# Window attention with routed experts on one core: half of the first slot's row transposes at the end of step 11, a shorter slot table placed ahead of the routing, no warming products in step 0, weight pieces from step 5

## The chip, the cores and the metric

The kernel runs on one core of one Trainium2 chip. The metric is the device time of one execution in microseconds (us); the median of three runs stands for the kernel. The engines are named as the profile names them: PE multiplies matrices (PEld loads its weights), DVE, ACT and POOL are the vector, scalar and general engines, and SP issues DMAs.

## The reference, cut to what matters

```python
# attention: batch 8, heads 8, seq 576, head_dim 64, window 64
scores = 1/sqrt(64) * q @ k.T
scores = where((0 <= row - col) & (row - col < 64), scores, -1e9)
attn = exp(scores - max); attn = attn / (sum(attn) + 1e-9)
x = (attn @ v)                       # 4608 tokens x 512
# one expert of 8 for every token
logits = x @ w_gate + modality_bias[modality_id]
e = argmax(logits); gate = softmax(logits)[e]
out = gate * (relu(x @ w1[e]) @ w2[e])   # w1: 512 x 1024, w2: 1024 x 512
```

## The kernel before, in words

The 4608 tokens are 36 pairs of 64-row blocks. A loop of 40 steps runs the attention as a software pipeline: step s holds the values (`values`, tile av) and the routing logits (`logits`) of earlier pairs, the scores (`scores`, tile sp) and row minima (`minima`, tile mn) of pair s, the transposes of the probabilities of pair s-1 (`probs_t`, PSUM to SBUF as pT by ACT), the transposes of the attention rows (`x_t`, xaT), the exponentials of pair s (`exps`, ACT), and the transposes of the next group's heads (`heads_t`, copied as kT and qT). All engines but the DMA rings work through orders that this code writes out by hand; the order of the calls is the order in each engine's queue.

Every second step a group of two pairs is routed: `route1` to `route3` put small DVE operations on a list, `routing`, and two indirect DMAs of POOL (`scatter`, line 735) write each token's row to a DRAM scratch tensor, xs_scratch, by expert. `tick` takes operations off that list, or off a second one, `queue`, which holds the *table*: tiny DVE operations on one partition that work out which rows the next expert *slot* may take. `plan` queues such a table for two slots after the groups named in `EARLY`; the first plan comes at the end of step 9 (group 2).

An expert slot is 256 token rows of one expert. Its work is cut into pieces by the generator `slot_pieces`, and from step `FIRST` = 12 on a step has four places for a piece (`gap`). The pieces of the first slot are: `x_part` 0 and 1 (four 128x128 transposes each of the slot's rows xt, line 255, then a split into a high part xh by ACT and a low part xl by DVE, lines 193 and 194), `first` k, i (12 products each into half of a PSUM bank, line 280; after i = 1 ACT makes hh and DVE makes hl of the bank, lines 288 and 289), and `second` (six products each, line 302). While the attention runs, `bank` gives every `first` the one bank em, and `x_part` 0 as well. So `first` 1, 0 can't write em before hh and hl of k = 0 have read it. `fetch` takes the next slot off `todo`: it ticks the table up to the operation that gives the slot's row number, SP reads that number (`load_slot`, line 202) and loads the rows into xt (line 204). Such a load is ordered behind the scatters of its groups.

The two most used experts' weights are kept as pairs Whi and Wlo. Each call of `weights` takes one piece a stage on: a load of 256 KB into a tile y by SP (lines 101 and 105), `split_hi` by ACT (line 112), `split_lo` by DVE in the call after it (line 117). 32 pieces are needed; `first` 0 and 1 use the first four of them. Before, the calls begin in step 3 (`WEIGHTS`).

In step 0, `keep_warm(4)` and later `keep_warm(3)` are products of zeros into the bank em (line 846), whose results nobody reads. The second of them stands behind the transposes of the first heads, which also go into em, and which DVE copies out as kT (line 563).

When the 40 steps are over, the pieces left run alone: loads, splits and products of further slots, and at the end one slot of 128 rows.

Of the kernel before, what the change touches and what calls it, by code (L numbers as in the profile page):

```python
# [8 lines left out]
F32 = mybir.dt.float32  # L9
# [4 lines left out]
ALU = mybir.AluOpType  # L14
# [5 lines left out]
P = 128  # L20
# [6 lines left out]
def tile_window_attn_moe(  # L27
# [12 lines left out]
    nc = tc.nc  # L40
# [13 lines left out]
    TP = 2 * P  # L54
# [6 lines left out]

    EARLY = ((2, (0, 1)), (4, (0, 1)), (6, (0, 1)), (8, (0, 1)), (9, (1, 2)), (10, (1, 2)), (11, (1, 2)),
             (12, (0, 2)), (13, (0, 2)), (15, (0, 2)))
    WEIGHTS = 3
    FIRST = 12


# [54 lines left out]
    queue = []  # L122
    issued = [0]
    n_raw = [0]
    routing = []
# [9 lines left out]
    def queued():  # L135
        return issued[0] + len(queue)

    def ts(pool, nm, in0, s1, op0, s2=None, op1=ALU.bypass, dtype=F32, out=None):
        t = pool.tile(list(in0.shape), dtype, name=nm) if out is None else out
        queue.append(lambda: nc.vector.tensor_scalar(  # L140
            out=t, in0=in0, scalar1=s1, scalar2=s2, op0=op0, op1=op1))
        return t

    def stt(pool, nm, in0, scalar, in1, op0, op1):
        t = pool.tile(list(in0.shape), F32, name=nm)
        queue.append(lambda: nc.vector.scalar_tensor_tensor(
            out=t, in0=in0, scalar=scalar, in1=in1, op0=op0, op1=op1))
        return t

    def tt(pool, nm, in0, in1, op, dtype=F32, out=None):  # L150
        t = pool.tile(list(in0.shape), dtype, name=nm) if out is None else out
        queue.append(lambda: nc.vector.tensor_tensor(out=t, in0=in0, in1=in1, op=op))
        return t
# [6 lines left out]
    def tiles_of(pool, nm, c, up, size):  # L160

        i = ts(pool, nm + "_i", c, float(size - 1) if up else 0.0, ALU.add, dtype=I32)
        sh = pool.tile(list(c.shape), I32, name=nm + "_s")
        queue.append(lambda: nc.vector.tensor_single_scalar(
            out=sh, in_=i, scalar=size.bit_length() - 1, op=ALU.arith_shift_right))
        return ts(pool, nm, sh, 0.0, ALU.add)
# [61 lines left out]
    def run_later():  # L228
        while later:
            later.pop(0)()  # L230

    def fetch():
        if fetched:
            return fetched.pop(0)
        row, late, buf, whichever, need = todo.pop(0)
        assert late is not None or not pads
        assert late is None or late in scattered
        tick(need - issued[0], table=True)
        nb = 1 if whichever == NANY else 2
        return dict(xt=load_slot(row, late, nb), buf=buf, any=whichever, nb=nb)  # L240
# [191 lines left out]
    def gap(it, wait=False):  # L432

        if next(it, "end") != "end" and not wait:
            run_later()
            tick()
# [40 lines left out]

    PARTS = ((K0, K1), (Q0, Q1))
    AHEAD = range(1, 8)
    WARM = 4, 3  # L480

    n_tp = [0]

    def turn_bank(s):

        i = n_tp[0]
        n_tp[0] += 1
        if s < FIRST and i % 5 > 1:
            return ps_m.tile([P, 512], F32, name=("em", "y0", "y1")[i % 5 - 2])
        return ps_t.tile([P, 512], F32, name="tp")  # L490
# [162 lines left out]
    def logits(p, lt):  # L653
        G, j = divmod(p, GB)
        xaT = st.pop((p, "xT"))
        for c in range(NC1):
            for i in range(2):
                cols = slice(c * P + i * W64, c * P + (i + 1) * W64)
                nc.tensor.matmul(  # L659
                    out=lt[i * W64:(i + 1) * W64, 0:E], lhsT=xaT[:, cols], rhs=wg[:, c, :],  # L660
                    start=(c == 0), stop=(c == NC1 - 1))
        if j == 0:
            st[G, "lg"] = small.tile(sh3, F32, name="lg")
        nc.vector.tensor_tensor(
            out=st[G, "lg"][:, j, :], in0=lt[:, 0:E], in1=bias_sel[:, p, :], op=ALU.add)
# [100 lines left out]
    def plan(T, xs_, cnt):  # L766

        nm = "e"
        xs_ = slice(*xs_)
        n = per_expert(pl, nm + "_n", tiles_of(pl, nm + "_f", cnt, False, TP), xs_)  # L770
        n = tt(pl, nm + "_av", n, used[-1][:, xs_], ALU.subtract)
        take = ts(pl, nm + "_take", n, 1.0, ALU.min)
        row = stt(pl, nm + "_first", used[-1][:, xs_], 2.0, base2[:, xs_], ALU.mult, ALU.add)
        row = tt(pl, nm + "_at", row, take, ALU.mult)
        rows = ts(tab, f"rows_{len(used)}", row, float(DUMMY), ALU.add, dtype=I32)
        new = pl.tile([1, 2], F32, name=nm + "_used")
        if xs_.stop - xs_.start < 2:
            ts(pl, nm, used[-1], 0.0, ALU.add, out=new)
        tt(pl, nm, used[-1][:, xs_], take, ALU.add, out=new[:, xs_])
        used.append(new)  # L780
        for i, x in enumerate(range(xs_.start, xs_.stop)):
            todo.append((rows[0:1, i:i + 1], f"scatter_after_{T}", x, None, queued()))

    def choose():

# [57 lines left out]
    def keep_warm(n):  # L843
        em = ps_m.tile([P, 512], F32, name="em")
        for _ in range(n):
            nc.tensor.matmul(out=em, lhsT=idle[:, 0:P], rhs=idle[:, 0:512], start=True, stop=True)

    keep_warm(WARM[0])
    ident_r = const.tile([P, P], F32R, name="ident_r")
    ident = ident_r.bitcast(F32)  # L850
    ident_0 = epool.tile([P, 512], F32, name="hl", bufs=2)[:, 0:P]
# [125 lines left out]
    for s in range(NPR + 4):  # L977
        j = s % GB
        for f, args in at.pop(s, ()):
            f(*args)  # L980
        n_tick = 6 if s < FIRST else 5
        n_gap = 0 if s < FIRST else 4
        G = s // GB + 1
        heads = PARTS[j] if G < NG else ()
        R = (s - 5) // GB if s >= 5 and j == 1 else -1
        if 1 <= s < FIRST:
            swap_upper(s - 1)

        if 2 <= s < NPR + 2:
            values(s - 2)  # L990
            values_out(s - 2)
        if 3 <= s < NPR + 3:
            logits(s - 3, turn_bank(s))
            if (s - 3) % GB == GB - 1:
                route1((s - 3) // GB)
        if s < NPR:
            scores(s)
            minima(s)
        if 1 <= s <= NPR:
            if s >= FIRST:  # L1000
                swap_upper(s - 1)
            swap_v(s - 1)
            for a in range(2):
                probs_t(s - 1, a, turn_bank(s))
            sums(s - 1)
        if s < NPR:
            exps(s, (0, 1))
        if s == 0:
            first_pair(1, (both[:1], both[1:]))
            keep_warm(WARM[1])  # L1010
            cast_bias()
        if n_gap > 0:
            gap(it, True)
        if 2 <= s < NPR + 2:
            x_t(s - 2, turn_bank(s))
        run_later()
        tick(2)
        if s == FIRST - 1:
            fetched.append(fetch())
        if s < NPR:  # L1020
            exps(s, (2, 3, 4))
        if n_gap > 0:
            if s < FIRST + 4 or s % 2:
                weights(s)
            gap(it, True)
        if heads:
            tp = turn_bank(s)
            heads_t(G, *heads[0], tp)
            heads_out(tp, G, *heads[0], nc.vector.tensor_copy)
        run_later()  # L1030
        tick(n_tick)
        cnt = None
        if R >= 0:
            tp = turn_bank(s)
            rk = route2(R, tp)
            if R == NG - 1 or any(R == T for T, _ in EARLY):
                cnt = counts_out(tab if R == NG - 1 else pl, counts(R, tp))
            route3(R, rk)
        if s < NPR:
            exps(s, (5, 6, 7))  # L1040
        if n_gap > 2:
            if FIRST < s < FIRST + 3:
                weights(s)
            gap(it, True)
        if heads:
            tp = turn_bank(s)
            heads_t(G, *heads[1], tp)
            heads_out(tp, G, *heads[1], nc.scalar.copy if heads[1] == K1 else nc.vector.tensor_copy)
        run_later()
        tick(n_tick)  # L1050
        if s == WEIGHTS:
            load_weights()
        if s >= WEIGHTS:
            weights(s)
        if n_gap > 3:
            gap(it, True)
        run_later()
        if s == 1:
            select_bias()
        if s == 4:  # L1060
            nc.sync.dma_start(out=xs_blk[DUMMY:DUMMY + 2].rearrange("b p c -> p b c"), in_=padrow)
        for T, xs_ in EARLY:
            if T == R:
                plan(T, xs_, cnt)
    tick(len(routing))
    tick(len(queue))

# [264 lines left out]
```

## Time and profile before

| what | value |
| --- | --- |
| median of 3 runs | 640.25 us (639.64 to 640.69) |
| the profiled execution | 639.68 us, of which its span is 637.9 us |
| granted clock in the page's rows | 9 of 9 tenths in all 40 slices |
| bytes moved by DMA | 88.07 MB, 138 GB/s over the span |

A row of the timeline gives the start and the length in us, the engine, the line, the operation, out<-in, how many were merged, and in brackets how long the engine stood idle before it and what ended that. In the windows view each row is a stretch with every engine's busy time. Starts of a step below are the starts of its scores on PE. The order views list an engine's instructions as they stand in its queue; no time is in them.

### The profile page before, as it was taken

The numbers are of one execution on the slowest core, as the hardware profiler recorded it, in microseconds if no ns is written. First come the engines' busy times: TensorE is split into PE (matmuls) and PEld (weight loads), VectorE is DVE, ScalarE is ACT, GpSimd is POOL, SyncE is SP. The second block draws the span as 40 slices with busy tenths as digits, with TensorE's granted clock in tenths as the row PEclk, the third lists the DMA queues.
The fourth block names the chain that finished last, engine by engine and source line by source line (L and its number), as shares of the span: only waits on it lengthen the run. The fifth ranks groups of instructions, "written<-read, shape, count | busy, mean of one in ns | idle before, by whom it ended". The sixth has DMA issues, their size and how long they took to land.

```text
span 637.9 us, 17255 instructions
## 1 busy us (share of the span) xinstructions
PE 618.2 (97%) x6508; PEld 555.2 (87%) x6509; DVE 366.2 (57%) x1489; ACT 299.4 (47%) x933; POOL 136.6 (21%) x315
## 2 busy tenths in 40 slices
PE   6999789999999999999999999999999999999996
PEld 4888688989898889889888899998999899989986
DVE  3899968776777766666654364213224624667611
ACT  3899876656656555646462111111112513554411
POOL 6333322132222320321222121011001101101202
PEclk9999999999999999999999999999999999999999
DMA  9999664775466543453312026312232723677300
GB/s 182 222 240 238 167 187 126 191 194 158 133 166 192 141 134 85 134 150 85 101 50 101 33 100 245 116 39 67 67 132 80 244 75 104 214 244 241 106 5 32
DMA packets 138773, 88.07 MB, mean 138 GB/s; under 512 B 116618, under 2 KB 116672, under 8 KB 138560
## 3 DMA queue, kind: packets, MB, share of 16 engines
q1 hardware_dynamic: 130112, 67.44, 40.2%
q0 software_dynamic: 5888, 18.93, 7.9%
q8 instruction: 52, 0.85, 0.6%
q10 hardware_dynamic: 2688, 0.58, 0.5%
q14 instruction: 33, 0.27, 0.1%
HBM read 67.49 MB, written 23.91 MB: 143 GB/s over the span
## 4 chain that ended last, share of the span: by engine, by line
PE 50%; DVE 0%; ACT 0%; issue 0%; POOL 0%; POOLq 0%; ACTq 0%
PE y L302 23%; PE em L280 13%; PE sp L280 10%; PE tp L440 1%; PE y L353 1%; PE av L634 1%; PE em L255 1%; PE tp L255 1%; PE sp L328 0%; PE em L328 0%; PE tp L659 0%; PE sp L582 0%; DVE xa L642 0%; ACT ss L608 0%; POOL out_dram L366 0%
## 5 line engine op out<-in xcount | busy, mean ns | idle before, releaser
L302 PE MATMUL y<-Whi,hh 128*128 128x512 f32 x288 | 118.7, 412 | 0.0
L608 ACT ACTIVATE ss<-ss,mn 128x128 f32<-128x128 f32 x288 | 112.6, 398 | 3.4 <-DVE mn L596 3.4
L302 PE MATMUL y<-Whi,hl 128*128 128x512 f32 x288 | 112.8, 392 | 0.0
L302 PE MATMUL y<-Wlo,hh 128*128 128x512 f32 x288 | 112.8, 392 | 0.0
L280 PE MATMUL em<-xh,Whi 128*128 128x256 f32 x400 | 102.9, 292 | 1.2 <-ACT xh L193 0.7
L280 PE MATMUL em<-xh,Wlo 128*128 128x256 f32 x400 | 98.1, 279 | 0.0
L289 DVE SCALAR_TENSOR_TENSOR hl<-em,hh 128x512 fp32r<-128x512 f32 x50 | 34.5, 690 | 91.4 <-ACT hh L288 91.3
L313 POOL DMA_INDIRECT out_dram<-y,id x36 | 37.3, 1037 | 222.6 <-DVE y L310 140.5
L280 PEld LDWEIGHTS em<-xh,Whi 128*128 128x128 f32 x400 | 75.4, 189 | 2.6 <-ACT xh L193 0.9
L280 PEld LDWEIGHTS em<-xh,Wlo 128*128 128x128 f32 x400 | 75.3, 188 | 0.9
L288 ACT ACTIVATE hh<-em 128x512 fp32r<-128x512 f32 x50 | 29.6, 591 | 93.0 <-PE em L280 89.1
L596 DVE CUSTOM_DVE_ANT_0 ss<-sp,masks 128x128 f32<-128x128 f32 x288 | 63.6, 286 | 11.4 <-PE sp L582 11.4
L617 ACT COPY pT<-tp 128x512 f32<-128x512 f32 x57 | 31.6, 589 | 76.3 <-PE tp L440 76.3
L302 PEld LDWEIGHTS y<-Whi,hl 128*128 128x128 f32 x288 | 54.1, 188 | 12.3
L280 PE MATMUL em<-xl,Whi 128*128 128x256 f32 x400 | 63.1, 279 | 0.0
L302 PEld LDWEIGHTS y<-Whi,hh 128*128 128x128 f32 x288 | 54.1, 188 | 7.3
L302 PEld LDWEIGHTS y<-Wlo,hh 128*128 128x128 f32 x288 | 54.3, 189 | 7.0
L608 ACT ACTIVATION_READ_ACCUMULATOR ss<-ss,mn 128x1 f32 x288 | 56.0, 195 | 0.0
L735 POOL DMA_INDIRECT xs_scratch<-xa,idx x36 | 36.3, 1010 | 84.8 <-DVE lm L678 26.9
L280 PEld LDWEIGHTS em<-xl,Whi 128*128 128x128 f32 x400 | 53.8, 188 | 0.0
L289 DVE SCALAR_TENSOR_TENSOR hl<-sp,hh 128x512 fp32r<-128x512 f32 x22 | 15.2, 692 | 60.8 <-ACT hh L288 60.8
L288 ACT ACTIVATE hh<-sp 128x512 fp32r<-128x512 f32 x22 | 13.1, 597 | 76.6 <-PE sp L280 76.6
(249 smaller groups left out, 1266.5 us busy)
## 6 DMA issues: line engine op xcount, KB each, us to landing
xt<-xs_scratch SPq DMA_DIRECT2D x18, 514.0 KB, 4.1
vo<-in_v_dram SPq DMA_DIRECT2D x32, 256.0 KB, 4.2
y<-in_moe_w_dram SPq DMA_DIRECT2D x32, 256.0 KB, 3.8
vo<-in_moe_w_dram SPq DMA_DIRECT2D x24, 256.0 KB, 3.8
ss<-in_moe_w_dram SPq DMA_DIRECT2D x24, 256.0 KB, 3.8
xs_scratch<-xs_scratch SPq DMA_DIRECT2D x8, 514.0 KB, 6.3
pT<-in_moe_w_dram SPq DMA_DIRECT2D x16, 256.0 KB, 3.5
qk<-in_k_dram SPq DMA_DIRECT2D x14, 256.0 KB, 4.5
```

The lines of the kernel that those rows point to most:

```text
L255: nc.tensor.transpose(out=tp[:, n * P:(n + 1) * P].bitcast(F32R), in_=xt[:, t, c * P:(c + 1) * P].bitcast(F32R), identity=ident_r)
L280: nc.tensor.matmul(out=hb[:, i * TP:(i + 1) * TP], lhsT=w[buf][:, c0:c0 + P], rhs=x[:, c * TP:(c + 1) * TP], start=(n == 0), stop=(n == le ...
L288: nc.scalar.activation(out=hh, in_=hb, func=AF.Relu),
L289: nc.vector.scalar_tensor_tensor(out=hl, in0=hb, scalar=0.0, in1=hh.bitcast(F32), op0=ALU.max, op1=ALU.subtract)))
L302: nc.tensor.matmul(out=sl["y", t], lhsT=h[:, i * TP + t * P:i * TP + (t + 1) * P], rhs=w[buf][:, c0:c0 + DM], start=(k == 0 and n == 0), s ...
L313: ins = nc.gpsimd.indirect_dma_start(out=out, out_offset=bass.IndirectOffsetOnAxis(ap=sl["id"][:, t:t + 1], axis=0), in_=y, in_offset=None ...
L353: nc.tensor.matmul(out=yp[:, cols], lhsT=sl["h", n][lo][:, c * P:(c + 1) * P], rhs=w[buf][:, c0 + cols.start:c0 + cols.stop], start=(m == ...
L440: nc.tensor.transpose(out=out_, in_=in_, identity=ident[p0:p0 + n, p0:p0 + n])
L596: nc.vector.tensor_tensor_reduce(out=ss[a][:, hp, :], in0=sp[a][:, hp * P:(hp + 1) * P], in1=mask, scale=-1.0 / 8.0, scalar=3.0e38, op0=AL ...
L608: nc.scalar.activation(out=ss[a][:, hp, :], in_=ss[a][:, hp, :], func=AF.Exp, bias=mn[:, h:h + 1], scale=-1.0, accum_out=sm[:, h:h + 1])
L617: nc.scalar.copy(out=pT, in_=pp)
L735: ins = nc.gpsimd.indirect_dma_start(out=xs, out_offset=bass.IndirectOffsetOnAxis(ap=idx[:, j:j + 1], axis=0), in_=xg[j], in_offset=None)
```

## The change

- The three warming products of step 0 go (`WARM`).
- The calls of `weights` begin in step 5 instead of 3; steps 12 and 15 get one more call each.
- `plan` is worked out with fewer operations: it compares the expert's count with 256 times the number of slots used, instead of first making whole slots of it. The row number comes ahead of the count of used slots. For the plan of step 9 the operations up to the row number are issued at once, where before they were ticked behind the routing's, in steps 10 and 11.
- `fetch` for the first slot stands at the start of step 11 and `x_part` 0 of that slot at its end; all later pieces come one place earlier. The logits of step 12 go to another bank.
- In the odd steps from 13 on the rest of the routing list is issued at the end of the step.

On PE, at the end of step 11 and in step 12, this stood before (ss are probabilities, xt the slot's rows, xa attention rows, Whi_64 heads of q and k, which lie in memory that later holds weights; Whi_65 and xh the first product's operands):

```order
L440 MATMUL tp<-ident_r,ss 128x128 x8
L255 MATMUL em<-ident_r,xt 128x128 x4
L440 MATMUL tp<-ident_r,xa_101 128x128 x4
L255 MATMUL tp<-ident_r,xt 128x128 x4
L440 MATMUL tp<-ident_r,Whi_64 128x128 x4
L280 MATMUL em<-xh,Whi_65 128x256
```

And this stands there now, at the end of step 11, with the values (av) of the next step behind it:

```order
L706 MATMUL em<-oh,ones 128x8
L440 MATMUL y_1731<-ident_r,Whi_64 128x128 x4
L255 MATMUL em<-ident_r,xt 128x128 x4
L634 MATMUL av<-ve,pT 64x64
L634 MATMUL av<-vo,pT 64x64
```

The first four transposes of the slot's rows moved from behind step 12's scores to a place ahead of step 12's values.

On PE at the end of step 12 the last products of `first` 0, 1 were followed before by the values of step 13:

```order
L280 MATMUL em<-xh,Whi_65 128x256
L280 MATMUL em<-xh,Wlo_66 128x256
L280 MATMUL em<-xl,Whi_65 128x256 x4
L634 MATMUL av<-ve,pT 64x64
L634 MATMUL av<-vo,pT 64x64
```

Now they are followed by one set of head transposes and then by `first` 1, 0, which writes the same bank:

```order
L280 MATMUL em<-xl,Whi_65 128x256 x4
L440 MATMUL tp<-ident_r,Whi_64 128x128 x4
L280 MATMUL em<-xh,Whi_65 128x256
L280 MATMUL em<-xh,Wlo_66 128x256
L280 MATMUL em<-xh,Whi_65 128x256
```

`first` 1, 0 came after the values, logits, scores and probabilities of step 13 before, and comes ahead of all of them now.

On DVE, the table of the first plan (names beginning with e_) stood in step 10 before, behind the routing's last operation and ahead of a split; four more operations of it followed in step 11:

```order
L691 TENSOR_REDUCE oh<-oh 128x8
L140 TENSOR_SCALAR e_f_i<-cnt 1x8
L164 TENSOR_SCALAR e_f_s<-e_f_i 1x8
L140 TENSOR_SCALAR e_f<-e_f_s 1x8
L152 TENSOR_TENSOR e_n_p<-sel_68,e_f 1x8
L157 TENSOR_REDUCE e_n<-e_n_p 1x1
L152 TENSOR_TENSOR e_av<-e_n,used_220 1x1
L140 TENSOR_SCALAR e_take<-e_av 1x1
L146 SCALAR_TENSOR_TENSOR e_first<-used_220,base_69 1x1
L117 TENSOR_TENSOR Wlo_66<-y,Whi_65 128x512
```

Now it stands at the end of step 9, behind the scatter's index and a split, and ahead of step 10's first operations:

```order
L747 CAST idx<-dst 128x2
L117 TENSOR_TENSOR Wlo_66<-y,Whi_65 128x512
L146 SCALAR_TENSOR_TENSOR e_first<-used_220,base_69 1x1
L152 TENSOR_TENSOR e_n_p<-sel_68,cnt 1x8
L157 TENSOR_REDUCE e_n<-e_n_p 1x1
L146 SCALAR_TENSOR_TENSOR e_av<-used_220,e_n 1x1
L146 SCALAR_TENSOR_TENSOR e_at<-e_av,e_first 1x1
L140 TENSOR_SCALAR rows_1471<-e_at 1x1
L512 COPY ve<-vo 64x512
L640 RECIPROCAL rs<-rs 128x8
```

The row number is there after six operations in step 9 instead of ten in steps 10 and 11; two operations for the slots used stay in step 10.

```diff
-    WEIGHTS = 3
+    WEIGHTS = 5
     FIRST = 12
...
-    WARM = 4, 3
+    WARM = 4
...
         xs_ = slice(*xs_)
-        n = per_expert(pl, nm + "_n", tiles_of(pl, nm + "_f", cnt, False, TP), xs_)
-        n = tt(pl, nm + "_av", n, used[-1][:, xs_], ALU.subtract)
-        take = ts(pl, nm + "_take", n, 1.0, ALU.min)
-        row = stt(pl, nm + "_first", used[-1][:, xs_], 2.0, base2[:, xs_], ALU.mult, ALU.add)
-        row = tt(pl, nm + "_at", row, take, ALU.mult)
+        was = used[-1][:, xs_]
+        row = stt(pl, nm + "_first", was, 2.0, base2[:, xs_], ALU.mult, ALU.add)
+        n = per_expert(pl, nm + "_n", cnt, xs_)
+        n = stt(pl, nm + "_av", was, -float(TP), n, ALU.mult, ALU.add)
+        row = stt(pl, nm + "_at", n, float(TP), row, ALU.is_ge, ALU.mult)
         rows = ts(tab, f"rows_{len(used)}", row, float(DUMMY), ALU.add, dtype=I32)
+        for i, x in enumerate(range(xs_.start, xs_.stop)):
+            todo.append((rows[0:1, i:i + 1], f"scatter_after_{T}", x, None, queued()))
...
-        tt(pl, nm, used[-1][:, xs_], take, ALU.add, out=new[:, xs_])
         used.append(new)
-        for i, x in enumerate(range(xs_.start, xs_.stop)):
-            todo.append((rows[0:1, i:i + 1], f"scatter_after_{T}", x, None, queued()))
+        new = new[:, xs_]
+        queue.append(lambda: nc.vector.scalar_tensor_tensor(
+            out=new, in0=n, scalar=float(TP), in1=was, op0=ALU.is_ge, op1=ALU.add))
...
             f(*args)
+        if s == FIRST - 1:
+            fetched.append(fetch())
...
-            logits(s - 3, turn_bank(s))
+            logits(s - 3, turn_bank(s) if s != FIRST else ps_m.tile([P, 512], F32, name="y0"))
...
             first_pair(1, (both[:1], both[1:]))
-            keep_warm(WARM[1])
             cast_bias()
         if n_gap > 0:
             gap(it, True)
+        if s == FIRST:
+            run_later()
...
-        if s == FIRST - 1:
-            fetched.append(fetch())
...
         if n_gap > 0:
-            if s < FIRST + 4 or s % 2:
+            if FIRST < s < FIRST + 4 or s % 2:
                 weights(s)
             gap(it, True)
+        if s == FIRST:
+            run_later()
+            weights(s)
...
         if n_gap > 2:
-            if FIRST < s < FIRST + 3:
+            if FIRST <= s < FIRST + 4:
                 weights(s)
             gap(it, True)
...
-        if n_gap > 3:
+        if n_gap > 3 or s == FIRST - 1:
             gap(it, True)
         run_later()
+        if s >= FIRST and j == 1:
+            tick(len(routing))
...
                 plan(T, xs_, cnt)
+                if not fetched and s < FIRST:
+                    tick(todo[0][-1] - issued[0], table=True)
```

More of the change, by code (lines that the diff above doesn't have):

```diff
@@ L846, in keep_warm @@
             nc.tensor.matmul(out=em, lhsT=idle[:, 0:P], rhs=idle[:, 0:512], start=True, stop=True)
-    keep_warm(WARM[0])
+    keep_warm(WARM)
     ident_r = const.tile([P, P], F32R, name="ident_r")
```

## The prediction

> **What bounds the kernel now.** I read the page first, then the busy time by step in windows, then PE's timeline at the start and around step 12, and last POOL's, SP's, ACT's and DVE's timelines at the places where PE waits.
>
> ```profile
> span 637.9 us, 17255 instructions
> PE 618.2 (97%) x6508; PEld 555.2 (87%) x6509; DVE 366.2 (57%) x1489; ACT 299.4 (47%) x933; POOL 136.6 (21%) x315
> ```
>
> PE is busy for 618.2 of 637.9 us. The change takes nothing but three products off PE, so what it can give lies in PE's 19.7 idle us and in stretches where PE goes at less than its pace. The windows, one for each step (columns: length; busy PE, PEld, DVE, ACT, POOL with counts; granted clock; DMA share; GB/s), show where those are.
>
> ```profile
> 26.89:31.76 4.87, 4.87 (x105) 4.51 (x101) 4.03 (x22) 4.72 (x19) 0.83 (x2) 1.00 0.86 222
> 42.08:47.45 5.37, 4.94 (x105) 4.51 (x101) 5.07 (x28) 5.37 (x23) 3.76 (x6) 1.00 0.98 244
> 70.33:76.87 6.54, 5.20 (x107) 4.59 (x104) 6.11 (x37) 5.45 (x21) 0.41 (x2) 1.00 0.39 106
> 76.87:89.33 12.46, 9.53 (x136) 8.14 (x132) 9.36 (x42) 9.52 (x33) 5.19 (x10) 1.00 0.75 216
> 89.33:100.01 10.68, 10.68 (x145) 9.62 (x141) 7.94 (x36) 6.78 (x23) 0.89 (x3) 1.00 0.37 102
> ```
>
> Step 3 (first row) is PE's alone. In step 6 (42.08) ACT is busy all the time and PE and DVE nearly so. In step 11 (70.33) DVE leads and PE is idle for 1.3 us; step 12 (76.87) holds 2.9 us of idle PE; from step 13 on PE has no gap. Everything that stands before 89 us moves the end one for one, everything later only if it makes PE wait.
>
> The start, on PE (columns: start, length, engine, line, operation, what, count, idle before):
>
> ```profile
> 8.71 1.98 PE L582 MATMUL sp<-kT,qT 64*64 64x128 f32 x32 [0.61 <-POOL hl L864]
> 11.96 0.63 PE L440 MATMUL y<-ident_r,qk 64*128 64x64 f32 x4
> 13.29 0.58 PE L846 MATMUL em<-hh 128*128 128x512 bf16 x1 [0.69 <-DVE X_mx L157]
> 14.10 0.63 PE L846 MATMUL em<-hh 128*128 128x512 bf16 x1 [0.22 <-issue]
> 14.52 1.06 PE L440 MATMUL y<-ident_r,Whi 128*128 128x128 f32 x4
> 16.36 1.99 PE L582 MATMUL sp<-kT,qT 64*64 64x128 f32 x32
> 18.28 0.81 PE L440 MATMUL tp<-ident_r,ss 128*128 128x128 f32 x4
> 18.92 0.60 PE L440 MATMUL em<-ident_r,ss 128*128 128x128 f32 x4
> 21.58 1.10 PE L582 MATMUL sp<-kT,qT 64*64 64x128 f32 x32
> ```
>
> The same 32 score products take 1.99 us at 16.36 and 1.10 us at 21.58, four transposes 1.06 and later 0.60: PE goes at about half pace until some 18.7 us, though the clock in the windows' rows reads 1.00 throughout. The pace changed after PE had been without a gap since 14.10, for 4.6 us.
>
> **The change, part by part.** The sum goes against the profiled execution, 639.68 us (639.68 - 637.9 = 1.8 outside the span), which lies 0.57 under the median of 640.25.
>
> *No warming products.* They wait for em and hold PE from 12.59 (11.96 + 0.63) to 14.52, 1.9 us. SP's last issue of the heads that the next transposes read, and its time to landing:
>
> ```profile
> 4.90 1.91 SPq L533 DMA_DIRECT2D Whi<-in_k_dram  x1
> DMA to landing us min/median/max: 6.3/6.3/6.3
> ```
>
> They are in memory at 11.2, so those transposes can start at 12.59. Without the products PE runs from 8.71 with no gap through the transposes and the scores of step 1. If the pace changes after as long a run as it did, 4.6 us, that is at 13.3 instead of 18.7, and the transposes and scores up to there are up to 0.9 us shorter each (1.99 - 1.10 for the scores). The bound on that side is 1.9 + 0.9 = 2.8. What is late next is POOL:
>
> ```profile
> 24.73 0.60 POOL L506 COPY ve<-vo 64x512 f32<-64x512 f32 x1
> ```
>
> This copy, which the second pair's values need, stands behind POOL's bias work, and that behind DVE's copies of the heads, which don't move as far as PE does; my estimate is that this gives about one such copy back, 0.6. So 2.2. If the pace still changes only at 18.7, eight probability transposes come before that and lose 2 x (1.06 - 0.60) = 0.9, and the gain is 1.0. I take -2.2, nearer to the early change because the run without a gap is longer than the one that sufficed. In steps 3 and later the gain persists, as PE there has nothing to wait for.
>
> The Trainium skill, "TensorE: Matmul & The Clock Gate", Part 1, says that the array runs at half clock until one free-running window of about 3.4 us was busy throughout; the trace agrees, and by that rule the change of pace would come between 12.1 and 15.5 us, and the gain would be -2.5 rather than -2.2, 637.9 in all.
>
> *Weights from step 5.* Two splits leave the crowded steps 5 and 6, which are alike, and return in steps 12 and 15. The groups of operations by line, from 30 to 60 us, give their price (count | busy, mean ns):
>
> ```profile
> L112 ACT CAST Whi<-y 128x512 fp32r<-128x512 f32 x5 | 3.2, 633 | 0.0
> L117 DVE TENSOR_TENSOR Wlo<-y,Whi 128x512 fp32r<-128x512 f32 x4 | 2.7, 684 | 0.0
> ```
>
> ACT has 2 x 0.5 to 0.6 us less, DVE 2 x 0.7. PE itself needs 4.87 (step 3) of step 6's 5.37, so at most 0.5 a step can be had: between 0 and -1.0, I take -0.6. Two 256 KB loads leave the stretch where the DMA share is near 1.0; that helps the heads' loads and costs nothing.
>
> *The shorter table.* Before, twelve operations lie in steps 10 and 11 (eight and four):
>
> ```profile
> 70.33 0.15 DVE L140 TENSOR_SCALAR e_f_i<-cnt 1x8 int32<-1x8 f32 x1
> 71.53 0.14 DVE L146 SCALAR_TENSOR_TENSOR e_first<-used,base 1x1 f32<-1x1 f32 x1
> 75.42 0.14 DVE L152 TENSOR_TENSOR e_at<-e_first,e_take 1x1 f32<-1x1 f32 x1
> 75.84 0.15 DVE L152 TENSOR_TENSOR e_used<-used,e_take 1x1 f32<-1x1 f32 x1
> ```
>
> They take 1.3 + 0.6 us of DVE. Six operations at the same pitch now delay step 10 by 0.9 and two more by 0.2. Of the first 1.3 that leaves 0.2, by which the end of step 11 comes earlier on PE; the row number is there at the end of step 9 instead of behind 75.42.
>
> *The early rows and transposes.* With the number early, the load of the rows waits for the scatters of its group. The second one's row in POOL's timeline, the line's time to landing, SP's issue and its landing:
>
> ```profile
> 67.19 0.97 POOL L735 DMA_INDIRECT xs_scratch<-xa,idx  x1 [0.28 <-POOL xa L734]
> DMA to landing us min/median/max: 5.3/5.7/6.1
> 76.73 0.39 SPq L204 DMA_DIRECT2D xt<-xs_scratch  x1
> DMA to landing us min/median/max: 3.7/3.7/3.7
> ```
>
> The scatter lands at 67.19 + 6.1 = 73.3, the rows 3.7 later, at 77.0 instead of 80.4. On PE:
>
> ```profile
> 75.37 0.27 PE L634 MATMUL av<-ve,pT 128*64 128x64 f32 x1
> 80.46 0.54 PE L255 MATMUL em<-ident_r,xt 128*128 128x128 f32 x4 [0.25 <-DMA xt<-xs_scratch]
> 83.40 0.39 PE L280 MATMUL em<-xh,Whi 128*128 128x256 f32 x1 [0.56 <-DVE xl L194]
> 84.82 0.39 PE L280 MATMUL em<-xh,Whi 128*128 128x256 f32 x1 [0.68 <-ACT xh L193]
> 87.83 0.27 PE L634 MATMUL av<-ve,pT 128*64 128x64 f32 x1
> ```
>
> The end of step 11, where the transposes now stand, is at 75.4, less 0.2; with SP's reaction the rows are there at 77.1: PE waits 1.9 us, ahead of step 12's values, logits and scores. From 77.1: transposes 0.4, values and logits 1.5 (87.83 to step 13's start at 89.33), scores 1.1, first probabilities 0.6; ACT gets them at 80.7. What ACT has to do from there up to hh, before, and, in rows by themselves, the page's group of the exponentials with a mean of 398 ns and two dozen products of `first` from the chain that ended last:
>
> ```profile
> 80.25 0.58 ACT L617 COPY pT<-tp 128x512 f32<-128x512 f32 x1 [1.04 <-PE tp L440]
> 86.53 0.62 ACT L547 COPY kT<-tp 128x512 f32<-128x512 f32 x1 [0.50 <-PE tp L440]
> 87.94 0.60 ACT L288 ACTIVATE hh<-em 128x512 fp32r<-128x512 f32 x1 [0.27 <-PE em L280]
> 88.57 0.69 DVE L289 SCALAR_TENSOR_TENSOR hl<-em,hh 128x512 fp32r<-128x512 f32 x1 [1.76 <-ACT hh L288]
> ```
>
> ```profile
> L608 ACT ACTIVATE ss<-ss,mn 128x128 f32<-128x128 f32 x288 | 112.6, 398 | 3.4 <-DVE mn L596 3.4
> ```
>
> ```profile
> 340.62 2.81 PE em L280 x24
> ```
>
> From 80.25 to 88.54 it is busy but for 0.50 and 0.27: 7.5 us. The order after has one pT more and one xh fewer in that stretch, so hh ends at 80.7 + 7.5 = 88.2 and hl at 88.9. Before, nobody waited for that, since `first` 1, 0 came after step 13's scores. Now it stands right behind `first` 0, 1, and PE gets there sooner: two pT of 0.5, two exponentials of 0.4, xh of 0.6 and xl of 0.7 take from 80.7 to 83.8, the low products left over 0.3, head transposes twice 0.4 and `first` 0, 1 a dozen products, 1.4, which is 86.3. So it waits 2.6 us. `first` 1, 0 is done at 90.3. Before, the same work was done by 87.83 + 1.4 = 89.2. So the waits of step 12 are exchanged for two longer ones: +1.1. The bounds are -0.8, if the rows are there when PE comes (1.9 less), and +2.1, if they land 1.0 later.
>
> *Everything later.* Pieces stand one place earlier. `x_part` 0 of later slots and `first` 1, 0 come nearer to the hl that frees em, with one `second` and two sets of head transposes between them; hh and hl take 1.3 (0.60 + 0.69). The few small waits at the turn of a slot come or go with it. I take 0; if they come to 0.2 a slot, six times, +1.2. The later tables and the routing's rest are off the path: DVE is busy 7.94 of step 13's 10.68.
>
> The sum: -2.2 - 0.6 + 1.1 + 0 = -1.7, so 638.0 by the profiled execution, 638.6 by the median. I forecast 638.2.
>
> **The rivals.** A: the pace changes at 18.7 as before. The start gives 1.0, the sum is -0.5: 639.4. For it: the score products before 11.96 brought no change, although PE was busy then as well. Against: there was a gap at 8.1 and one at 12.6.
>
> B: the rows don't hold up PE, because the scatters land sooner with less DMA traffic, or steps 10 and 11 are longer than I count. The wait of 1.9 falls away: 636.3. For it: of the scatters' 6.1 a part may be the loads of heads beside them. Against: both scatters took over 5, and those loads stay.
>
> C: the bank em makes PE wait once in each later slot, 6 x 0.2 = 1.2: 639.4. Against: the cover is longer than hh and hl; for it: ACT has other work ahead of hh.
>
> D, slower: the three products, and not the transposes, are what brings the pace. Then it comes only after the first real products that follow, the values at about 20 at half pace, and 4.6 us behind them, near 24.6. From 18.7 to there PE does 5.9 us of work at 1.10/1.99 of its pace and loses 2.6 us against A: -0.5 + 2.6 = +2.1, 641.8 to 642.3. It decides if the pace changes later than some 23 us. For it: after the four products at the start no change came, and three later it did. Against: the last product ended 4 us before it. The same page of the Trainium skill, Part 4, says that transposes don't count as busy for the clock, which speaks against this change; the rows here can't part the two.
>
> **How the numbers follow.** A difference of 0.2%, 1.3 us, is about what a measurement of this kernel can tell from none. The forecast has 0.42, B 0.18, A 0.20, C 0.10, D 0.08; 0.02 is left for what I don't see. The forecast and B are faster by over 1.3, A and C within, D slower: 0.60, 0.31, 0.09. The range reaches from B (636.3) and half a microsecond beyond to short of D, taking in +1.0 for late rows: 635.8 to 640.8. Most of the chance being of one sign, no second range is needed.
>
> **What would show it.** Right: scores of step 1 near 14.3 us and four transposes at 0.60 soon after; an idle PE of about 2 us ahead of the first `x_part`, put down to the xt load; another of 2 to 3 us ahead of `first` 1, 0, put down to hl; step 13's values, now behind `first` 1, 0, at about 90.3 - 2.8 = 87.5, and no gap from there. Wrong: long transposes beyond 20 us (D), no wait for xt (B), new waits for hl in every fourth step (C).

## The result, and the profile after

| kernel | median us | ratio to the kernel before, on the same chip | 95% interval |
| --- | --- | --- | --- |
| before (4 runs beside the changed one) | 640.47 | 1 | |
| changed | 657.35 (653.97 to 658.30) | 1.0242 | 1.0223 to 1.0261 |

By this ratio the change costs 2.4%, some 15.5 us (by the two medians 16.9); the forecast was a gain of 2. The profiled execution is the fastest of the four, 653.97 us. Its page:

```profile
span 652.2 us, 17224 instructions
PE 623.0 (96%) x6506; PEld 557.9 (86%) x6506; DVE 357.8 (55%) x1449; ACT 297.3 (46%) x933; POOL 139.1 (21%) x315
PEclk9999989999999999999999999999999999999999
```

PE's idle time has grown from 19.7 to 29.2 us, and its busy time by 4.8 us though it does three products less; one slice of the clock row shows 8. The windows by step (steps 3, 6, 11, 12, 13, 14, then two stretches of 2 us; columns as before):

```profile
25.01:29.88 4.87, 4.87 (x105) 4.51 (x101) 4.03 (x22) 4.58 (x19) 0.84 (x2) 1.00 0.92 197
39.73:45.41 5.68, 4.93 (x104) 4.50 (x100) 5.34 (x28) 4.97 (x23) 3.73 (x6) 1.00 1.05 284
68.32:76.25 7.93, 5.71 (x111) 4.99 (x108) 6.88 (x37) 7.74 (x29) 1.50 (x3) 1.00 0.91 229
76.25:92.08 15.83, 12.91 (x144) 11.08 (x140) 8.82 (x35) 7.75 (x26) 3.70 (x10) 0.89 0.52 150
92.08:102.72 10.64, 10.64 (x144) 9.63 (x140) 7.60 (x36) 6.79 (x23) 0.12 (x1) 1.00 0.27 65
102.72:116.20 13.48, 10.98 (x140) 9.47 (x136) 8.09 (x40) 7.51 (x25) 4.77 (x10) 1.00 0.67 194
88.00:90.00 2.00, 2.00 (x14) 1.78 (x15) 0.13 (x2) 0.00 (x0) 0.00 (x0) 0.54 0.97 219
90.00:92.00 2.00, 2.00 (x48) 2.00 (x46) 0.19 (x1) 0.00 (x0) 0.00 (x0) 0.61 1.11 281
```

Step 12 has a granted clock of 0.89, and the last two rows show where: 0.54 and 0.61 from 88 to 92 us. Step 14, which took 10.48 us before (100.01 to 110.49), takes 13.48, and 2.5 of it PE is idle. On PE's timeline, the start (scores of steps 1 and 2, and four transposes between them), and the waits of steps 11, 12 and 14:

```profile
14.47 1.99 PE L582 MATMUL sp<-kT,qT 64*64 64x128 f32 x32
16.90 0.60 PE L440 MATMUL em<-ident_r,ss 128*128 128x128 f32 x4
19.56 1.10 PE L582 MATMUL sp<-kT,qT 64*64 64x128 f32 x32
74.31 0.51 PE L255 MATMUL em<-ident_r,xt 128*128 128x128 f32 x4 [1.59 <-DVE tgt L722]
87.47 0.39 PE L280 MATMUL em<-xh,Whi 128*128 128x256 f32 x1 [2.13 <-DVE hl L289]
110.36 0.51 PE L302 MATMUL y<-Wlo,hh 128*128 128x512 f32 x1 [2.39 <-DVE Wlo L117]
```

The start is 1.9 to 2.0 us sooner. The first two waits were forecast (1.9 and 2.6 us); that for a low part Wlo was not. The releaser named for the first, tgt, doesn't bear on these transposes: DVE's last reading of em (line 716) ended at 73.46. The rows' load, issued at 70.39, was the late one; in e3, e6 and e9 the trace names it.

Step 28 shows what goes on later: POOL, PE, DVE's first minimum and ACT's copies of the probabilities.

```profile
260.78 1.06 POOL L313 DMA_INDIRECT out_dram<-y,id  x1 [13.66 <-DVE rs L640]
262.32 0.98 POOL L735 DMA_INDIRECT xs_scratch<-xa,idx  x1 [0.28 <-POOL xa L734]
263.78 0.98 POOL L735 DMA_INDIRECT xs_scratch<-xa,idx  x1 [0.28 <-issue]
260.81 1.10 PE L582 MATMUL sp<-kT,qT 64*64 64x128 f32 x32
261.84 1.09 PE L440 MATMUL tp<-ident_r,ss 128*128 128x128 f32 x8
264.46 0.29 DVE L596 CUSTOM_DVE_ANT_0 ss<-sp,masks 128x128 f32<-128x128 f32 x1 [2.93 <-remote]
265.22 1.07 ACT L617 COPY pT<-tp 128x512 f32<-128x512 f32 x2 [7.07 <-remote]
265.86 0.66 PE L440 MATMUL tp<-ident_r,xa 128*128 128x128 f32 x4 [1.51 <-ACT pT L617]
```

The scores end at 261.91 and the transposes at 262.93, but DVE and ACT start on them at 264.46 and 265.22: the hand-over is 2.55 us late while three indirect DMAs of POOL follow each other, and PE then waits 1.51. Before, minima started 0.05 us behind the scores in 18 of the 23 steps from 13 on, and POOL's scatters stood in the middle of a step. Step 28 before (scores, first minimum, POOL's next indirect DMA):

```profile
252.11 1.10 PE L582 MATMUL sp<-kT,qT 64*64 64x128 f32 x32
253.26 0.29 DVE L596 CUSTOM_DVE_ANT_0 ss<-sp,masks 128x128 f32<-128x128 f32 x1 [0.27 <-PE sp L582]
256.68 1.05 POOL L313 DMA_INDIRECT out_dram<-y,id  x1 [7.95 <-DVE lm L678]
```

### The profile page after: what moved, and what is told of

Its sections match the earlier page's. It is cut to its first block, busy times and chain, and to the rows that moved or that the text cites. A ratio compares the mean times of both kernels' runs of the same rounds, so it can differ in the third digit from the quotient of the medians.

```text
span 652.2 us, 17224 instructions
## 1 busy us (share of the span) xinstructions
PE 623.0 (96%) x6506; PEld 557.9 (86%) x6506; DVE 357.8 (55%) x1449; ACT 297.3 (46%) x933; POOL 139.1 (21%) x315
## 4 chain that ended last, share of the span: by engine, by line
PE 70%; another core or an unknown queue 2%; ACT 2%; DMA 2%; SPq 2%; DVE 1%; issue 1%; POOL 0%; POOLq 0%; ACTq 0%
PE y L302 26%; PE em L280 18%; PE sp L280 9%; PE tp L440 7%; PE av L634 3%; PE sp L582 3%; PE tp L659 1%; DMA xs_scratch<-xs_scratch 1%; PE em L255 1%; PE y L353 1%; DVE hl L289 1%; PE tp L255 1%; SPq L1100 1%; SPq L1099 1%
```

## The experiments

Each ran beside the kernel before on one chip. Where nothing else is said the edit is to the changed kernel.

**e1, no warming products** (edit to the kernel before).

```diff
-            keep_warm(WARM[1])
```

> The kernel before without the three warming products, nothing else changed. In the changed kernel step 1's scores began 1.9 us sooner and step 9's 2.5 us sooner. Theory 'start': these products are what held the start back, so this kernel is 2.0 to 2.5 us faster than the 640.5 of the kernel before, 638.0 to 638.5. Rival 'weights': half of it or more came from the weights that begin in step 5, then 639.0 to 639.5. Rival D of the prediction (the pace comes late without them): 641.8 to 642.3.

Measured 639.08 against 641.75: 0.9966 (0.9953 to 0.9979), 2.2 us faster. The products held up the start; rival D of the prediction is out.

**e2, the routing's rest alone** (edit to the kernel before).

```diff
+        if s >= FIRST and j == 1:
+            tick(len(routing))
```

> The kernel before with one addition: in the odd steps from 13 on the rest of the routing list is issued at the end of the step, so that POOL's two scatters stand at the start of the even step. Theory 'scatters at the hand-over': while they run, PE's results reach DVE and ACT late (1.8 to 2.9 us in the changed kernel's steps 14, 18, 22, 28, 32), and PE pays for it: 5 to 10 us slower than 640.5, 645 to 650. Rival 'early pieces': the scatters cost nothing by themselves and only the pieces one place earlier leave no slack: 640 to 641.

Measured 642.64 against 641.75: 1.0015 (1.0000 to 1.0030), some 1.0 us, at the edge of what can be told. The hand-over is late here too, in step 28 by 1.03 us, but PE's next transposes of attention rows come with no wait, behind a `second`:

```profile
253.10 1.07 POOL L735 DMA_INDIRECT xs_scratch<-xa,idx  x1 [14.18 <-DVE rs L640]
254.45 0.29 DVE L596 CUSTOM_DVE_ANT_0 ss<-sp,masks 128x128 f32<-128x128 f32 x1 [1.19 <-PE tp L440]
255.66 0.60 PE L440 MATMUL tp<-ident_r,xa 128*128 128x128 f32 x4
```

**e3, weights from step 3.**

```diff
-    WEIGHTS = 5
+    WEIGHTS = 3
```

> The changed kernel with the weights' calls from step 3 again (its later calls stay). Theory 'late weights': the 2.4 us for which PE waits in step 14 for a low part Wlo go, and steps 5 and 6 cost 0.4 to 0.6 more: about 655.5 against 657.3. Rival 'the low part is late because DVE is': its operations are held up in step 14 by the minima, not by the order of the pieces: unchanged or 0.5 slower, 657 to 658.

Measured 652.45 against 641.75: 1.0166 (1.0133 to 1.0198), some 5 us under the changed kernel, more than either theory. Step 14 has no wait for a Wlo:

```profile
105.87:116.70 10.83, 10.70 (x140) 9.55 (x136) 8.00 (x40) 6.78 (x24) 4.38 (x7) 1.00 0.65 172
```

**e4, the routing's rest one place earlier.**

```diff
-        tick(n_tick)
+        tick(len(routing) if s >= FIRST and j == 1 else n_tick)
...
-        if s >= FIRST and j == 1:
-            tick(len(routing))
```

> The changed kernel, but the rest of the routing list is issued one place earlier in the odd steps, ahead of the last weights call and the last piece, so that POOL's scatters run 1.5 to 3 us before the next step's scores are handed over. Theory 'scatters at the hand-over': the late hand-overs of steps 14, 18, 22, 28, 32 go, and with them most of what was lost after step 13: 648 to 651. Rival 'early pieces': the same waits stay, 656 to 658.

Measured 659.96 against 641.75: 1.0286 (1.0259 to 1.0313), no better. It didn't take the scatters away from the hand-over: in step 28 they start at 267.48, with the scores at 267.55, and the minima wait even longer:

```profile
267.48 1.05 POOL L735 DMA_INDIRECT xs_scratch<-xa,idx  x1 [13.50 <-DVE rs L640]
267.55 1.10 PE L582 MATMUL sp<-kT,qT 64*64 64x128 f32 x32
271.89 0.29 DVE L596 CUSTOM_DVE_ANT_0 ss<-sp,masks 128x128 f32<-128x128 f32 x1 [3.60 <-remote]
```

**e5, the pieces in their old places.** With this go the extra logits bank and the weights' moved calls (neither is shown here).

```diff
-        if n_gap > 3 or s == FIRST - 1:
+        if n_gap > 3:
             gap(it, True)
```

> The changed kernel with the pieces back in their old places (first half of the transposes behind step 12's scores); no warming products, weights from step 5, the short table and the routing's rest at the end of odd steps stay. Theory 'early pieces': nearly all of the loss hangs on the places, so 640 to 642 (2.2 gained at the start, 1.0 lost by the routing's rest as in the run with it alone, and up to 2 by the weights). Rival 'weights and routing': the late weights make PE wait wherever the pieces are, 645 to 650.

Measured 638.34 against 640.25: 0.9966 (0.9955 to 0.9978). All the loss, and more, is gone; the routing's rest and the later weights are cheap without the early pieces. The rival falls.

**e6, the scatters behind the hand-over.** In place of the two lines of e2, in the even steps behind the first exponentials:

```diff
             exps(s, (0, 1))
+        while s > FIRST and j == 0 and routing and f"scatter_after_{(s - 6) // GB}" not in scattered:
+            tick()
```

> The changed kernel, but the routing's rest is issued in the even steps behind the minima and the first two exponentials, so that POOL's scatters start after the scores and the first transposes have been handed over. Theory 'scatters hold the hand-over': DVE's minima and ACT's copies of the probabilities no longer wait 1.8 to 2.9 us in steps 14, 18, 22, 28 and 32; the waits of 1.5 us of PE in steps 28 and 32 go, and so may step 14's for the weights: 651 to 654 against 657 to 659. Rival 'places alone': DVE and ACT are late by their own work, and the waits stay, 657 to 659.

Measured 647.30 against 640.25: 1.0106 (1.0079 to 1.0133), 8.7 us less than the changed kernel (0.0136 of 640). Step 28 again:

```profile
261.46 1.06 POOL L313 DMA_INDIRECT out_dram<-y,id  x1 [13.29 <-DVE rs L640]
261.47 1.10 PE L582 MATMUL sp<-kT,qT 64*64 64x128 f32 x32
266.21 1.05 POOL L735 DMA_INDIRECT xs_scratch<-xa,idx  x1 [2.49 <-DVE lg L679]
262.99 0.29 DVE L596 CUSTOM_DVE_ANT_0 ss<-sp,masks 128x128 f32<-128x128 f32 x1 [0.85 <-PE tp L440]
263.19 1.07 ACT L617 COPY pT<-tp 128x512 f32<-128x512 f32 x2 [4.36 <-PE tp L440]
264.83 0.60 PE L440 MATMUL tp<-ident_r,xa 128*128 128x128 f32 x4
```

The minima come 0.42 us behind the scores' end (262.57), and PE doesn't wait. One out store is left beside the scores; that it holds the minima isn't shown, since in e14's step 28 the same store at the same place goes with 0.05. In steps 14, 18 and 22 they are back at 0.05. The wait for a Wlo in step 14 stayed, 1.92 us: it is not of the late hand-over's making. By the two profiles the changed kernel is 0.8 us longer than this one in step 14 and 7.0 us longer from step 16 to step 35, of which steps 28 and 32 have 3.8.

The six executions of this kernel differ with the clock: 644.38 us at a mean granted clock of 1.000, 645.50 at 0.997, 647.10 at 0.993, 647.50 at 0.992, 649.49 at 0.987 (the profiled one) and 650.56 at 0.985.

**e7, unread products in the two waits of PE.** `fill(n)` is n products of ones, 128x512, into the bank y1, which holds nothing then.

```diff
+        if 8 and s == FIRST:
+            fill(8)
+        if 4 and s == FIRST - 1:
+            fill(4)
         if n_gap > 3 or s == FIRST - 1:
             gap(it, True)
```

> The changed kernel with products that nobody reads in the two waits of PE that it has around step 12: four of 128x512 in front of the first transposes, eight in front of the third piece of the first product, into a bank that is free. Theory 'idleness drops the clock': the granted clock of 0.5 to 0.6 from 88 to 92 us goes and 2 us with it; the timed runs come closer together: 654 to 656 against 657 to 659. Rival 'the clock drops by itself': same drop, same time.

Measured 652.57 against 640.25: 1.0190 (1.0176 to 1.0204), half a per cent, 3.3 us, under the changed kernel. PE waits 0.41 us instead of 2.13, and the clock stays at 1.00 behind it; but it falls to 0.50 at another place, behind a wait of 2.81 us in step 11 for which the trace names no releaser. The profiled execution is the slowest of the six (657.60 us; the others 651.91 to 653.02), so that drop needn't be in them. First the wait, then the windows:

```profile
92.76 0.38 PE L280 MATMUL em<-xh,Whi 128*128 128x256 f32 x1 [0.41 <-DVE hl L289]
```

```profile
94.00:96.00 2.00, 2.00 (x56) 1.84 (x58) 0.41 (x1) 0.00 (x0) 0.00 (x0) 1.00 1.02 231
74.00:76.00 2.00, 2.00 (x10) 1.99 (x10) 0.93 (x8) 0.68 (x2) 0.00 (x0) 0.50 0.35 47
```

**e8, no warming products and the short table** (edit to the kernel before: e1's line, the change's `plan`, and its first table issued at once).

```diff
-            keep_warm(WARM[1])
...
                 plan(T, xs_, cnt)
+                if not fetched and s < FIRST:
+                    tick(todo[0][-1] - issued[0], table=True)
```

> The kernel before without the three warming products and with the short table, whose first row number is worked out at the end of step 9; weights from step 3, pieces and routing as before. If the parts add up: 2.2 for the start and 0.2 to 1 for the table, 638.0 to 639.3 against 640.5 to 641.7 of the kernel before. Rival 'the table delays step 10': six operations ahead of step 10's first ones, no gain beyond the start's: 639 to 640.5.

Measured 637.32 against 640.25: 0.9971 (0.9950 to 0.9991). The table adds nothing that can be told from e1.

**e9, e6 with the weights from step 3**, and **e10, the same with e7's products.** Both put earlier edits together:

```diff
-    WEIGHTS = 5
+    WEIGHTS = 3
...
+        if 8 and s == FIRST:
+            fill(8)
+        if 4 and s == FIRST - 1:
+            fill(4)
```

The lines below the dots are in e10 alone.

> The changed kernel with the scatters behind the hand-over (as in e6) and the weights from step 3 (as in e3); the pieces stay early. If the three losses add up: e6 gave 647.3, the wait of 1.9 us for a low part Wlo in its step 14 goes and with it at times a drop of the clock: 643 to 645, still 3 or more above the 640.3 of the kernel before, the rest being the waits around step 12 and the clock behind them. Rival 'one cause': with the scatters moved the weights don't matter, 647.

> As e9, and with the unread products of e7 in the two waits of step 12. Theory 'idleness drops the clock': the granted clock stays near 1.00 from 74 to 98 us, 2 to 4 us less than e9: 640 to 642. Rival 'the clock drops by itself': as e9, 643 to 645.

Measured 648.35 and 647.46 against 640.66: 1.0122 (1.0107 to 1.0137) and 1.0105 (1.0092 to 1.0118). The losses don't add up: the wait for Wlo is gone, and a wait in step 15 stands in its place. In e9 ACT stands idle for 6.08 us ahead of a weight's split, ACT's copies of the probabilities are queued behind it, and PE waits for them; the clock falls behind that (e9's windows). The trace names no releaser of the split. The likely one is the weight's load: three of them were issued from 115.07 on.

```profile
120.38 0.62 ACT L112 CAST Whi<-y 128x512 fp32r<-128x512 f32 x1 [6.08 <-issue]
120.90 1.06 ACT L617 COPY pT<-tp 128x512 f32<-128x512 f32 x2
121.53 1.02 PE L440 MATMUL tp<-ident_r,xa 128*128 128x128 f32 x4 [2.34 <-ACT pT L617]
```

```profile
122.00:124.00 2.00, 2.00 (x7) 1.67 (x6) 0.24 (x1) 2.00 (x8) 0.00 (x0) 0.50 0.88 213
```

In e10 that wait is 3.62 us, and no drop of the clock shows in its profile at all. In time the two can't be told apart, so the price of the clock is not settled by them.

**e11, e5 with the routing's rest as before.**

```diff
-        if s >= FIRST and j == 1:
-            tick(len(routing))
```

> The pieces in their old places and the routing's rest where it was, with the change's other parts: no warming products, weights from step 5, short table. By e5 (638.3) and e2 (the routing's rest alone +1.0): 637.3. Against e8 (637.3, weights from step 3) it prices the later weights: between 636.5 (a gain of 0.8) and 637.8.

Measured 637.60 against 640.66: 0.9947 (0.9934 to 0.9960), the lowest ratio of all, 3.4 us faster than the kernel before; the intervals of e1, e5, e8 and e13 overlap with it. Against e8 the later weights gain 0.2%, which the intervals don't part from nothing.

**e12, e6 with copies on POOL at the end of the odd steps.**

```diff
                 nc.vector.reciprocal(out=xg[j][:, DM:DM + 1], in_=se[:, j:j + 1])
+            for _ in range(14 if G >= 4 else 0):
+                nc.gpsimd.tensor_copy(out=busy, in_=xg[1][:, DM - 63:DM + 1])
```

> As e6 (scatters behind the hand-over), with 14 copies of 128x64 on POOL at the end of every odd step from 13 on, where the changed kernel's scatters stand, 2 to 3 us of POOL's time. Theory 'the scatters hold PE's reports': POOL's being busy is harmless, DVE's minima and ACT's copies come as in e6, about 647 to 648. Rival 'a busy POOL at that place does it': late hand-overs and waits as in the changed kernel, 652 or more.

Measured 651.14 against 640.66: 1.0173 (1.0160 to 1.0186), between the two theories. In step 14 POOL is busy across the scores, and the minima come 0.05 us behind them (102.01 + 1.10 = 103.11; 103.17):

```profile
100.50 4.50 POOL L731 COPY busy<-xa 128x64 f32<-128x64 f32 x14 [15.57 <-DVE xa L729]
102.01 1.10 PE L582 MATMUL sp<-kT,qT 64*64 64x128 f32 x32
103.17 0.29 DVE L596 CUSTOM_DVE_ANT_0 ss<-sp,masks 128x128 f32<-128x128 f32 x1 [0.67 <-PE sp L582]
```

So a POOL that is merely busy doesn't delay the hand-over there; its indirect DMAs at that place do. What the copies cost comes elsewhere: by the profiles steps 16, 20, 24, 28 and 32 are 3.0 us longer together than in e6.

**e13, the first transposes alone early**, with e11's routing: the first place of step 12 stays empty, all other pieces are in their old places. The extra logits bank and the weights' moved calls stay as in the changed kernel.

```diff
-        if n_gap > 0:
+        if n_gap > 0 and s != FIRST:
             gap(it, True)
```

> As e11 (old places, routing's rest as before), but the first half of the transposes alone stands at the end of step 11; the first place of step 12 is left empty, so every later piece keeps its old place. Theory 'the pieces behind': the transposes at the end of step 11 make PE wait 1.5 to 3 us there and spare as much in step 12, so 637 to 639, like e11. Rival 'the transposes': the wait for the rows, and the clock behind it, is the greater part of e6's loss: 642 to 645.

Measured 636.96 against 640.25: 0.9963 (0.9943 to 0.9983). By itself the early half of the transposes costs nothing and gives nothing that can be told from e11: PE waits 1.66 us for the rows and spares about that much in step 12.

```profile
74.68 0.50 PE L255 MATMUL em<-ident_r,xt 128*128 128x128 f32 x4 [1.66 <-DVE se L723]
```

**e14, all pieces but those transposes early**, else as e6.

```diff
+            run_later()
+            gap(it, True)
             run_later()
...
-        if n_gap > 3 or s == FIRST - 1:
+        if n_gap > 3:
```

> As e6 (scatters behind the hand-over), but the first half of the transposes stands in step 12 again, together with the second half in its first place; every later piece stays one place early. Theory 'the pieces behind': PE still waits about 2 us for hl in step 12 and 2 us for a Wlo in step 14, with the clock falling behind them: 643 to 647. Rival 'the transposes': without the wait at the end of step 11 most of e6's loss goes: 638 to 641.

Measured 643.19 against 640.25: 1.0044 (1.0028 to 1.0061), 6.2 us above e11. The scatters' place doesn't part the two: in the profiles they start 4.3 to 7.0 us behind the start of the scores in e14's even steps from 14 on, 4.3 to 7.6 in e11's. Both waits are there, and the clock falls behind the first:

```profile
85.88 0.38 PE L280 MATMUL em<-xh,Whi 128*128 128x256 f32 x1 [1.91 <-DVE hl L289]
107.93 0.50 PE L302 MATMUL y<-Wlo,hh 128*128 128x512 f32 x1 [1.92 <-DVE Wlo L117]
```

```profile
86.00:88.00 2.00, 2.00 (x11) 2.00 (x12) 0.53 (x2) 0.00 (x0) 0.00 (x0) 0.54 0.79 192
```

## Why the prediction was wrong

With ratios taken times 640, the kernels form a ladder: 640.0 before; 636.6 with the start, the weights and the table (e11); 642.8 with the pieces behind the transposes, and the `weights` calls that go with them, one place early (e14, +6.2); 646.8 with the transposes early too (e6, +4.0); 655.5 with the routing's rest at the end of the odd steps (the changed kernel, +8.7).

*The start, -2.2: right in size, wrong in its working.* e1 gives 2.2 (1.3 to 3.0). But the pace didn't change at 13.3: the scores at 14.47 still took 1.99 us, and transposes of 0.60 stand behind them, at 16.90. The gain is the products' 1.9 and not the early change less a copy of POOL. Transposes ran without a gap from 10.67 to 14.47 and brought no change; two more microseconds of scores did. The Trainium skill, "TensorE: Matmul & The Clock Gate", Part 4, says that transposes don't count as busy for the clock in the same way, and these rows agree with it rather than with Part 1's window taken alone. What brings the change stays open, and its place isn't the kernel's own: e10 and e5 issue the same up to there, but e10's scores of step 1 already take 1.42 us, while e5's take 1.99 and the transposes behind them are still slow (1.06 us for the four at 17.57). So the early change that the -2.2 counted on comes in some executions and not in others, and the agreement in size is in part luck.

*Weights and table, -0.6 and -0.2:* e11 against e1 gives 1.2 for both (0.0019 of 640, with intervals that overlap), which agrees with the 0.8 but can't be told from nothing.

*The early rows and transposes, +1.1 with bounds of -0.8 and +2.1: this step failed.* Its two waits came as told, 1.59 and 2.13 us for 1.9 and 2.6. Yet from step 11's start to step 13's the profile has 23.8 us instead of 19.0; `first` 1, 0, which moved in, is 1.4 of that, which leaves +3.4. The bound of -0.8 also left out the bank: em is free at 73.46, so PE, done at 72.72, would have waited 0.7 us even for rows that were there. What the step left out otherwise is threefold. First, the later pieces also need the weights a place earlier, while the weights start two steps later; I priced the later weights by the steps that they leave and not by the pieces that need them, and PE waits 1.9 to 2.4 us for a Wlo in step 14. Second, behind a wait of 2 us the clock is often halved, for 3.4 us in the changed kernel's profile and in e14's, for 10.2 behind e6's wait of 3.27; half of 3.4 is 1.7 us, by this estimate nearly the wait again. Third, the pad rows are issued later against a slot's pieces (at 402.22, 3.3 us behind a slot's first transposes; in e11 0.4 ahead of them), and the next rows' load, behind them on SP, comes too late, so PE waits some 1.5 us there (in e6 and e14 too, not in e11). SP's and PE's rows of the changed kernel:

```profile
402.22 10.68 SPq L1100 DMA_DIRECT2D xs_scratch<-xs_scratch  x8
419.70 0.40 SPq L204 DMA_DIRECT2D xt<-xs_scratch  x1
423.58 0.50 PE L255 MATMUL em<-ident_r,xt 128*128 128x128 f32 x4 [1.54 <-DMA xt<-xs_scratch]
```

Together the early pieces cost 10.2 us (e6 against e11) where the prediction had +1.1.

*"Everything later ... I take 0": for the pieces nearly right.* From step 16's start to step 35's e14's profile takes 205.2 us and e11's 204.2, a loss of 1.0 where I gave 0 to 1.2; to the end it is 1.7.

*"The later tables and the routing's rest are off the path": this step failed too, and it is the largest single rung of the ladder.* I looked at DVE's load and not at POOL's two scatters behind it, which moved from the middle of a step to the scores' hand-over. That costs about 1 in the old places (e2 1.0; e5 against e11 1.2) and 8.7 with the early pieces, where the term had been put at nothing. With the early pieces the out store falls to the end of the odd step: in steps 28 and 32 three indirect DMAs in a row (260.78 to 264.76) hold the hand-over longer than the one piece behind it covers. By the profiles those two steps lose 3.8 us against e6; most of the rest is spread over the other even steps, and in some of them PE itself is slower (see the last section).

None of the rivals had the mechanism; D, the only one on the slow side, stood at the wrong place. Open remain two things. One is why the transposes cost 4.0 on top of the early pieces (e6, with a wait of 3.27 us) and nothing alone (e13, 1.66). The wait for the rows is 1.4 to 1.7 us in some profiles and 3.2 to 3.4 in others, and this doesn't look like the edit's making: e6 issues the same as the changed kernel up to there, but its load is issued 6.8 us behind the second scatter instead of 5.8, and its rows take 4.6 instead of 3.9. A part of the 4.0 goes with the clock: e6's execution at a clock of 1.000 took 644.38, 1.2 above e14's median. The other is by what path POOL's indirect DMAs delay DVE and ACT.

## What to carry to other kernels

When a change issues a list of operations earlier, follow each operation to the queue that it ends in, DMAs above all, and ask what is handed over at that moment. Shifting all pieces by one place moves every deadline of theirs, so check each input (weights, rows, banks) against its new due time, also where the same change delays it. A wait of PE of 2 us or more should be priced twice, since the clock may go with it; single parts that gain are worth running without the rest.

## What the runs showed of the hardware

The granted clock falls to half after shorter waits than I would have thought. In the profiles of all sixteen kernels, counting PE's gaps of over 1.0 us between 25 and 600 us, none of 37 gaps under 1.8 us was followed by a drop, 8 of 14 gaps of 1.8 to 2.5 us were, and 4 of 5 longer ones; e5 and e11 show one drop each without such a gap, where step 12 has four waits of 0.5 to 0.7 close together (other kernels have these waits and no drop). A drop lasted 3.4, 6.8 or 10.2 us. The Trainium skill, "TensorE: Matmul & The Clock Gate", "Why this matters for your kernels", advises against idle gaps of over about 3 us; these traces put the threshold lower, near 2 us, and the outcome differs from run to run. That fits the spread of the changed kernel's times (654 to 658, with mean clocks of 0.997 to 0.987) and of e6's (644 to 651, 1.000 to 0.985).

While POOL issues indirect DMAs as PE ends a group of products, DVE and ACT start on it late. In the changed kernel's even steps the minima come 0.4 to 1.8 us behind the scores with two such DMAs around them (1.8 in steps 14, 18 and 22, 1.1 in 34, 0.4 and 0.55 in 26 and 30) and 1.9 and 2.55 with three (32 and 28), against 0.05 in most steps without one. PE goes on in most of these steps, but not in all: where a scatter starts some 0.7 us ahead of the scores, the 32 score products themselves take 1.3 to 1.9 us instead of 1.10, with the granted clock at 1.00 (steps 30 and 34 of e2 and of the changed kernel; in no step from 13 on of the kernels whose scatters stand elsewhere). Step 30 of e2:

```profile
272.81 1.07 POOL L735 DMA_INDIRECT xs_scratch<-xa,idx  x1 [7.04 <-DVE rs L640]
273.50 1.91 PE L582 MATMUL sp<-kT,qT 64*64 64x128 f32 x32
```
